# Two transformer-mixer layers on one core: VectorE's exponentials begin during layer 0's feed, and its first phase covers 1024 queries

## The chip, the cores and the metric

One NeuronCore of a Trainium2 chip runs the whole program. The metric is device time in microseconds (us), the median of several runs. The engines are TensorE (PE, with its weight loads PEld), VectorE (DVE), ScalarE (ACT), GpSimd (POOL) and SyncE (SP, which issues most DMAs). Each runs its own list of instructions in order, and waits on semaphores for the others.

## The reference

Two equal layers over x of 2048 tokens by 640, in bf16. Each layer adds attention with 32 heads of width 20 to x, and then a mixer, an MLP that works across tokens.

```python
def _A_ref(x, wqkv, wo):
    qkv = (x @ wqkv).reshape(B, S, 3, H, Dh).transpose(2, 0, 3, 1, 4)
    q, k, v = qkv[0], qkv[1], qkv[2]
    p = softmax(einsum("bhqd,bhkd->bhqk", q, k) * Dh ** -0.5)
    return einsum("bhqk,bhkd->bhqd", p, v).transpose(0, 2, 1, 3).reshape(B, S, D) @ wo

def _B_ref(x, w1, b1, w2, b2):
    u = gelu(einsum("bsd,sf->bdf", layernorm(x), w1) + b1)
    return (einsum("bdf,fs->bds", u, w2) + b2).transpose(0, 2, 1)

for _ in range(2):
    x = x + _A_ref(layernorm(x), A_wqkv, A_wo)
    x = x + _B_ref(layernorm(x), B_w1, B_b1, B_w2, B_b2)
```

The scores are 32 x 2048 x 2048 in each layer, and every one needs an exponential.

## The kernel before

**Units and chunks.** Heads go in 8 groups of 4, queries in 4 blocks of 512, keys in 16 tiles of 128. A unit is one block of queries, one group and one tile of keys; it has four chunks, one a head, of 128 keys by 512 queries. A layer has 4·8·16 = 512 units and so 2048 chunks. (In the last block a chunk is cut into two halves of 256 queries over two key tiles; the count is the same.)

**Two ways to an exponential.** PE writes scores (line 687, function `s_matmul`) into PSUM tiles S of three and of two chunks in turn, and ACT turns a whole tile into P with one instruction (line 757, `emit_exp`). Or PE writes one chunk into the PSUM bank Dt, and DVE makes the exponential with integer arithmetic (`ve_admit`, `ve_enqueue`): line 547 moves the chunk into the tile ew, two chunks make a pair, and a pair goes through a shift (line 645, mostly on POOL), a square (line 577), a product (line 581, tile et) and the last step into Pd (line 600, or line 598 where POOL has prepared its first part in line 628). The value products of P and Pd (line 1310) are summed in the PSUM bank acc.

**The planner.** No order is written by hand. While the kernel is built, a loop in `attention` keeps modelled clocks for PE, DVE and ACT, and a coarser one for POOL (`port`), and appends each instruction to its engine's list when the model says that it fits. Score tiles are issued so that ACT never waits; value products and "fills" (projections, transposes, output projection, mixer) go into the gaps, and where nothing is ready PE multiplies zeros (line 746) to keep its clock. `ve_admit` puts a chunk on DVE if DVE's modelled backlog is under 7 us, at least four units ahead of ACT, with a margin of 3.0 us (`VE_MARGIN`) between the planned result and its use. POOL's part runs beside a DVE instruction chosen as host (`ve_shift`, `ve_base`).

**The feed and the early phase.** Layer 0 begins with `TokenFeed`: x is loaded by tiles of 128 tokens, normalized on DVE, transposed on PE, and projected into K, Q and V for the first four groups. Keys appear one block of 512 tokens after another, so no unit order is fixed yet: `extend` picks units from `early_runs`, the early query blocks times four groups, as far as their keys and queries are there (`reach`). Whenever a run is broken off, the sum in acc is transposed (line 794) and kept in KT's rows of groups that are not used yet, and added later (line 802). Once all the keys of the early runs are there, the order of the remaining units is fixed. `early_qbs = (0,)` makes this phase 64 units long in layer 0, `(0, 1)` 128 units, as in layer 1 (`MixFeed`).

**The end of the feed.** `feed_ended` closes the feed's buffers, opens the next ones (`open_late`, among them the four pools of DVE's exponentials: vew, vet, vey, vep) and calls `after_end`: POOL clears the padded output weights wo_pad (line 1481) and issues two small bias loads (lines 182 and 183), SP loads wo_pad with 32 DMAs (line 200), and the second half of V becomes a fill. `ve_admit` does nothing before, as its first condition asks for `late`, nor while the early phase still lasts (`early[0]`).

In layer 1 the feed is the mixer of layer 0, and a last mixer ends the program.

Of the kernel before, what the change touches and what calls it, by code (L numbers as in the profile page):

```python
# [12 lines left out]
BF16 = mybir.dt.bfloat16  # L13
F32 = mybir.dt.float32
I32 = mybir.dt.int32
I16 = mybir.dt.int16
U16 = mybir.dt.uint16
F16 = mybir.dt.float16
# [44 lines left out]
POOL_HOST = 0.45  # L63
POOL_BASE_HOST = 0.45
VEP_BUFS = 4
VE_ADD = (1.22, 1.03, 0.69)
POOL_DMA = 0.9

# [12 lines left out]
def kernel(  # L81
# [141 lines left out]
    def attention(st, x_in_ap, x_mid, uacc_l, feed, feed_stack):  # L223
# [11 lines left out]
            return pp[f"s{w}"].tile([128, w, 512], F32, name="S")  # L235
        ntmp, ptp = st.ntmp, st.ptp
        p1.enter_context(tc.manual_schedule(engines={nc.vector.engine, nc.scalar.engine, nc.gpsimd.engine}))
        late = {}

        def open_late():  # L240
            def pool(name, bufs):
                late[name] = p1.enter_context(tc.tile_pool(name=f"{name}{layer}", bufs=bufs, reuse_waits="tile"))
            pool("xsp", 3 if x_in_ap.dtype == F32 else 2)
            pool("w1sp", 2)
            pool("ustg", 2)
            pool("atp", NG + 4)
            pool("vew", 3)
            pool("vet", 1)
            pool("vey", 2)
            pool("vep", VEP_BUFS)  # L250
        T2 = ntmp.tile([128, 16, 32], BF16, name="T2")
        nc.gpsimd.memset(T2[:], 0.0)
        h2_tiles, tt_state, attnT_tiles = {}, {}, {}
# [250 lines left out]
        def located(n):  # L504
            return cursor[0] >= NH * (n + 1)

        ve_w, ve_P, ve_ready, ve_users, ve_procs = {}, {}, {}, {}, deque()
        ve_state = dict(unit=-1, pair=0, slot=0)

        def ve_admit(t):  # L510
            now = pem["t"] - WAVE
            if (not late or early[0] or cursor[0] >= NCH or Dbank.free > now + 0.02 or
                    backlog(now) > CFG["VE_BACKLOG"]):
                return
            p, slot = ve_state["pair"], ve_state["slot"]
            if slot == 0:
                if len(ve_procs) > 2:
                    return
                done = backlog(now) + 2 * 1.2 + 4.0 + CFG["VE_MARGIN"]
                n = max(cursor[0] // NH + max(CFG["VE_LEAST"], math.ceil(done / 1.8)), ve_state["unit"] + 1)  # L520
                if n >= NU:
                    n = max(cursor[0] // NH + math.ceil((done - CFG["VE_MARGIN"]) / 1.8), ve_state["unit"] + 1)
                if n >= NU and Dbank not in banks:
                    banks.append(Dbank)
                if n >= NU or not unit_ok(units[n], now - 0.1):
                    return
                ve_state["unit"] = n
            n = ve_state["unit"]
            js = {c[1] for c in tiles[t]}
            free = [j for j in range(NH) if (n, j) not in on_dve]  # L530
            c = (n, next((j for j in free if j not in js), free[0]))
            clash = c[1] in js
            on_dve.add(c)
            loc[c] = (p, slot)
            ve_users.setdefault(p, []).append(c)
            ve_shifted.setdefault(p, [])
            Dt = Dbank.alloc()
            s_matmul(Dt[:, :], *c)
            at = pe_wave("S", cells=0.25) if clash else now
            Dbank.free = 1e9  # L540
            if slot == 0:
                ve_w[p] = late["vew"].tile([128, 2, 512], I32, name="ew")
            w = ve_w[p]

            def first(end):
                Dbank.free = end + DVE_TO_PE
                nc.vector.tensor_scalar(out=w[:, slot, :], in0=Dt[:, :], scalar1=127.0 * FIX,  # L547
                                        scalar2=0.0, op0=ALU.add, op1=ALU.max)

            def firsted(end):  # L550
                pieces.append((p, slot, w, end))
                bases.append((p, slot, w, end))
                if slot == 1:
                    ve_enqueue(p, 2, end + DVE_NEXT)
            submit(Proc(2, [(0.69, first, 0.0)], at + PE_TO_DVE, after=firsted))
            ve_state["slot"] = 1 - slot
            if slot == 1:
                ve_state["pair"] = p + 1

        def ve_enqueue(p, k, ready):  # L560
            w = ve_w.pop(p)
            wh = w[:, 0:k, :].rearrange("p a b -> p (a b)").bitcast(I16).rearrange("p (c two) -> p c two", two=2)
            frac = wh[:, :, 0].bitcast(U16)
            whole = wh[:, :, 1]
            box = {}

            def shifted(end):
                todo = [x for x in range(k) if x not in ve_shifted[p]]
                c0, c1 = 512 * todo[0], 512 * (todo[-1] + 1)
                for x in list(pieces):  # L570
                    if x[0] == p:
                        pieces.remove(x)
                shift(nc.vector, ve_y_of(p)[:, c0:c1], frac[:, c0:c1])

            def squared(end):
                y = ve_y_of(p)[:, 0:512 * k]
                nc.vector.tensor_tensor(out=y, in0=y, in1=y, op=ALU.mult)  # L577

            def mantissa(end):
                box["t"] = late["vet"].tile([128, 1024], I16, name="et")  # L580
                nc.vector.scalar_tensor_tensor(out=box["t"][:, 0:512 * k], in0=ve_y.pop(p)[:, 0:512 * k],  # L581
                                               scalar=MANT_C * MANT_K ** 2, in1=frac, op0=ALU.add, op1=ALU.mult)

            def expo(end):
                Pd = ve_result(p)
                ve_P[p] = Pd
                ve_ready[p] = end + DVE_TO_PE
                ve_procs.popleft()
                for x in [x for x in bases if x[0] == p]:
                    bases.remove(x)  # L590
                based = ve_based.pop(p, [])
                parts = [range(k)] if len(based) in (0, k) else [[x] for x in range(k)]
                for part in parts:
                    lo, hi = 512 * part[0], 512 * (part[-1] + 1)
                    bits = Pd[:, 0:k, :].rearrange("p a b -> p (a b)").bitcast(I16)[:, lo:hi]
                    t = box["t"][:, lo:hi]
                    if part[0] in based:
                        nc.vector.tensor_tensor(out=bits, in0=bits, in1=t, op=ALU.add)  # L598
                    else:
                        nc.vector.scalar_tensor_tensor(out=bits, in0=whole[:, lo:hi], scalar=128.0, in1=t,  # L600
                                                       op0=ALU.mult, op1=ALU.add)
            steps = [(0.15 + 0.27 * (k - len(ve_shifted[p])), shifted, 0.0, True)] if len(ve_shifted[p]) < k else []
            cost = VE_ADD[min(2, len(ve_based.get(p, [])) + 2 - k)]
            steps += [(0.69, squared, 0.0, True), (1.22, mantissa, 0.0, True), (cost, expo, 0.0, True)]
            proc = Proc(4, steps, ready, allow=lambda me: ve_procs[0] is me and
                        (len(me.steps) > 1 or p in ve_results or p - VEP_BUFS not in ve_users))
            proc.pair, proc.ready = p, max([ready] + ve_shifted_at.get(p, []))
            ve_procs.append(proc)
            dvm["procs"].append(proc)
# [2 lines left out]

        def ve_result(p):
            if p not in ve_results:
                ve_results[p] = late["vep"].tile([128, 2, 512], BF16, name="Pd")
            return ve_results[p]

        def ve_base(at):
# [19 lines left out]

        def ve_y_of(p):
            if p not in ve_y:  # L640
                ve_y[p] = late["vey"].tile([128, 1024], F16, name="ey")
            return ve_y[p]

        def shift(engine, out_ap, in_ap):
# [754 lines left out]
        for k_, v_ in dict(dvm=dvm, acm=acm, pem=pem, Proc=Proc, submit=submit, ln_proc=ln_proc, t_fill=t_fill,  # L1399
                           add_fill=add_fill, when=when, v_fill=v_fill, proj_fill=proj_fill, enqueue_qproj=enqueue_qproj,  # L1400
                           kready=kready, vready=vready, base=base, rest=rest, tready=tready, s_start=s_start, KT=KT,
                           Dbank=Dbank, misc=misc, spare=spare, warm_bank=warm_bank, acc_free=acc_free, pe_wave=pe_wave,
                           pump=pump, open_psum=open_psum, tables=[]).items():
            setattr(cx, k_, v_)
        feed.begin(cx)
        feed_ended()
        t = 0
# [44 lines left out]

    class TokenFeed:
        groups = 4
        early_qbs = (0,)
        act_helps = True
        act_free = 0.0
        warm_until = 5.6
# [115 lines left out]
    class MixFeed:  # L1574
        groups = 4
        early_qbs = (0, 1)
        act_helps = True
        act_free = 0.0
        warm_until = 0.0
# [283 lines left out]
```

## Time and profile before

| what | value |
|---|---|
| median of 3 runs | 1757.26 us (1757.2 to 1757.28) |
| the profiled execution | 1757.27 us |
| its span, first to last instruction | 1755.5 us |
| granted clock of TensorE | 1.0 |
| instructions in the span | 43109 |
| layer 0: first exponential on ACT starts, last one ends | 16.05 us, 819.9 us |
| layer 1: first exponential on ACT starts | 856.46 us |
| first exponential step on DVE starts | 109.43 us |

The profile is one execution. "Busy" counts the time in which an engine runs an instruction, waits excluded; a group's line gives the source line, engine, operation, tiles written and read, the count, and after the bars the busy time with the mean of one instruction in ns, and the idle time ahead of them with what ended most of it. In the table of stages each row has the stretch, its length, then busy us and count of instructions for PE, PEld, DVE, ACT and POOL, the granted clock, the share of the DMA engines and GB/s. A row of the order of time has the start, the duration and, in square brackets, the idle time before it.

### The profile page before, as it was taken

The page shows a single profiled execution, that of the slowest core. Times are in us where ns is not written, and L with a number is a line of the kernel's source. Part 1 is how long each engine was busy: PE and PEld are TensorE (multiplying, and loading weights), DVE is VectorE, ACT ScalarE, POOL GpSimd, SP SyncE. Part 2 cuts the span into 40 slices and gives each one's busy share as a digit, 9 for nine tenths or more (in the row PEclk, how much of TensorE's full clock was granted, in tenths as well). Part 3 has the DMA queues.
Part 4 walks back from the last instruction along what each step waited for, and adds up shares of the span by engine and source line. Part 5 has one row for each costly group of instructions (what it writes and reads, how often), then busy time and mean ns, then how long its engine had stood idle before and what let it go on. Part 6 is the DMA issues. An engine that isn't in the chain of part 4 may idle for free.

```text
span 1755.5 us, 43109 instructions
## 1 busy us (share of the span) xinstructions
PE 1670.5 (95%) x17783; PEld 666.8 (38%) x17864; DVE 1521.2 (87%) x2468; ACT 1668.4 (95%) x1502; POOL 577.3 (33%) x921
## 2 busy tenths in 40 slices
PE   8999999999999999999999999999999999999999
PEld 3333233333333344444444433233333333444455
DVE  7479999999999999998543469999999999999973
ACT  8999999999999999999779999999999999999970
POOL 2124442343444343342000023434434442434310
PEclk9999999999999999999999999999999999999999
DMA  4200000000112100133322100001001220101445
GB/s 117 37 4 1 1 1 2 20 28 2 35 53 82 39 25 25 39 86 108 116 78 74 55 21 1 1 2 39 24 1 61 82 72 9 62 2 40 120 124 176
DMA packets 103013, 81.85 MB, mean 47 GB/s; under 512 B 50976, under 2 KB 87456, under 8 KB 102816
## 3 DMA queue, kind: packets, MB, share of 16 engines
q1 hardware_dynamic: 97280, 71.22, 13.7%
q0 software_dynamic: 5536, 7.88, 1.5%
q8 instruction: 139, 2.28, 0.6%
q14 instruction: 58, 0.48, 0.1%
HBM read 55.48 MB, written 23.59 MB: 45 GB/s over the span
## 4 chain that ended last, share of the span: by engine, by line
ACT 50%; PE 24%; issue 21%; DVE 3%; POOL 0%; DMA 0%; another core or an unknown queue 0%; SPq 0%; ACTq 0%; POOLq 0%; DVEq 0%
ACT P L757 50%; PE S L687 7%; PE acc L1310 3%; PE misc L1052 2%; PE ya L1746 2%; PE acc L746 2%; PE misc L1161 1%; PE misc L1101 1%; PE um L1733 1%; PE ya L1755 1%; DVE et L581 1%; DVE ew L547 1%; PE yb L1746 1%; PE misc L1665 0%; PE Dt L1161 0%
## 5 line engine op out<-in xcount | busy, mean ns | idle before, releaser
L757 ACT ACTIVATE P<-S 128x1536 bf16<-128x1536 f32 (+2 forms) x1434 | 1620.8, 1374 | 13.2 <-PE S L687 12.7
L687 PE MATMUL S<-QTq,KT 32*128 32x512 bf16 (+1 forms) x4452 | 577.5, 337 | 65.2 <-ACT P L757 47.1
L645 POOL TENSOR_SCALAR ey<-ew 128x512 f16<-128x512 uint16 x515 | 318.2, 618 | 727.3 <-DVE et L581 323.4
L687 PEld LDWEIGHTS <-KT 32*128 32x128 bf16 x5124 | 233.2, 91 | 524.9 <-issue 497.2
L547 DVE TENSOR_SCALAR ew<-Dt 128x512 int32<-128x512 f32 x516 | 351.5, 681 | 19.8 <-PE Dt L687 13.6
L1310 PE MATMUL acc<-P,Vaug 128*32 128x512 bf16 (+1 forms) x4448 | 363.5, 343 | 0.3 <-DVE Vaug L367 0.3
L746 PE MATMUL acc<-zr,zw 128*32 128x512 bf16 x4232 | 325.5, 382 | 1.2 <-POOL zr L154 1.2
L581 DVE SCALAR_TENSOR_TENSOR et<-ey,ew 128x1024 int16<-128x1024 f16 x258 | 321.4, 1246 | 2.9
L628 POOL TENSOR_SCALAR Pd<-ew 128x512 int16<-128x512 int16 x303 | 186.4, 619 | 142.3 <-DVE et L581 37.4
L687 PE MATMUL Dt<-QTq,KT 32*128 32x512 bf16 (+1 forms) x672 | 198.2, 332 | 0.0
L577 DVE TENSOR_TENSOR ey<-ey 128x1024 f16<-128x1024 f16 x258 | 184.4, 715 | 0.5
L1310 PEld LDWEIGHTS <-Vaug 128*32 128x32 bf16 x5120 | 102.4, 94 | 176.7 <-issue 162.4
L746 PEld LDWEIGHTS <-zw 128*32 128x32 bf16 x4452 | 110.8, 96 | 96.1 <-issue 50.9
L600 DVE SCALAR_TENSOR_TENSOR Pd<-ew,et 128x1024 int16<-128x1024 int16 (+1 forms) x138 | 138.2, 1002 | 0.3
L598 DVE TENSOR_TENSOR Pd<-Pd,et 128x1024 int16<-128x1024 int16 (+1 forms) x183 | 117.1, 640 | 6.3 <-POOL Pd L628 3.8
L887 POOL TENSOR_TENSOR rstd<-veps,mhalf 128x1 f32<-128x1 f32 x60 | 47.6, 793 | 227.0 <-DVE veps L885 197.3
L1310 PE MATMUL acc<-Pd,Vaug 128*32 128x512 bf16 (+1 forms) x672 | 101.3, 334 | 1.2 <-DVE Pd L598 1.2
L1161 PE MATMUL misc<-hh,wq_pad 128*128 128x512 bf16 x273 | 82.4, 383 | 2.6 <-issue 1.7
L1052 PEld LDWEIGHTS <-w1st 128*128 128x128 bf16 x672 | 52.8, 97 | 57.8 <-issue 45.2
L794 DVE STREAM_TRANSPOSE T<-acc 128x512 f32<-128x512 f32 (+1 forms) x81 | 56.4, 696 | 20.3 <-PE acc L1310 19.8
L1101 PE MATMUL misc<-wo_pad,attnT 128*128 128x320 bf16 x384 | 73.0, 302 | 0.5 <-DVE QTq L369 0.3
L1052 PE MATMUL misc<-x1last,w1st 128*128 128x320 bf16 x384 | 72.9, 302 | 0.0
(145 smaller groups left out, 1184.2 us busy)
## 6 DMA issues: line engine op xcount, KB each, us to landing
w2s<-in_B_w_dram SPq DMA_DIRECT2D x16, 768.0 KB
uacc<-ustg POOLq DMA_DIRECT2D x24, 320.0 KB, 2.6
x1in<-xd SPq DMA_DIRECT2D x24, 320.0 KB
w1st<-in_B_w_dram SPq DMA_DIRECT2D x24, 256.0 KB
xd<-x2s SPq DMA_DIRECT2D x16, 320.0 KB
xin<-xd SPq DMA_DIRECT2D x16, 320.0 KB
w1st<-in_B_w_dram SPq DMA_DIRECT2D x24, 192.0 KB
xd<-x1s SPq DMA_DIRECT2D x12, 320.0 KB
```

Source lines behind the costliest of these rows:

```text
L547: nc.vector.tensor_scalar(out=w[:, slot, :], in0=Dt[:, :], scalar1=127.0 * FIX, scalar2=0.0, op0=ALU.add, op1=ALU.max)
L577: nc.vector.tensor_tensor(out=y, in0=y, in1=y, op=ALU.mult)
L581: nc.vector.scalar_tensor_tensor(out=box["t"][:, 0:512 * k], in0=ve_y.pop(p)[:, 0:512 * k], scalar=MANT_C * MANT_K ** 2, in1=frac, op0=ALU ...
L598: nc.vector.tensor_tensor(out=bits, in0=bits, in1=t, op=ALU.add)
L600: nc.vector.scalar_tensor_tensor(out=bits, in0=whole[:, lo:hi], scalar=128.0, in1=t, op0=ALU.mult, op1=ALU.add)
L628: after_vector(nc.gpsimd.tensor_scalar(out=bits, in0=whole, scalar1=128.0, scalar2=0.0, op0=ALU.mult, op1=ALU.add))
L645: return engine.tensor_scalar(out=out_ap, in0=in_ap, scalar1=MANT_K / FIX, scalar2=-MANT_K * MANT_S, op0=ALU.mult, op1=ALU.add)
L687: pe(nc.tensor.matmul(out_ap[:, c0:c0 + w], lhsT=KT[32 * j:32 * j + 32, g, kt * 128:(kt + 1) * 128], rhs=get_QT(st, qb)[32 * j:32 * j + 32 ...
L746: pe(nc.tensor.matmul(bank[32 * j:32 * j + 32, 0:w], lhsT=zw[:], rhs=zr[:, :, 0:64].to_broadcast([128, w // 64, 64]), start=start, stop=st ...
L757: nc.scalar.activation(out=P[:, 0:ncs, :].rearrange("p a b -> p (a b)"), in_=St[:, 0:ncs, :].rearrange("p a b -> p (a b)"), func=ACT.Exp, ...
L1052: pe(nc.tensor.matmul(t[:, 0:w], lhsT=w1_of[(p, ft)][:, sti, :], rhs=rows_in[sti][:, c0:c1], start=(sti == 0), stop=(sti == n_in - 1)))
L1310: pe(nc.tensor.matmul(acc[32 * j:32 * j + 32, a0:a0 + w], lhsT=Vaug[:, (kt * H + hh_) * VW:(kt * H + hh_) * VW + 32], rhs=P[:, slot, c0:c0 ...
```

## The change

Three things in layer 0. The four pools of DVE's exponentials are opened ahead of the feed, at the other end of SBUF (`side="right"`), and `ve_admit` asks for them in place of `late`. While the early phase lasts, DVE may take a unit that is not yet in the list: the new function `far` lets the list be extended up to it, if at least six units more than that (`VE_SPARE`) can be reached. And `early_qbs` of `TokenFeed` becomes `(0, 1)`. For layer 1 the flag `ve_early` is off; its pools are opened where they were, at the other end of SBUF.

```diff
+VE_SPARE = 6
...
-        late = {}
+        late, ve = {}, {}
+
+        def open_ve():
+            for name, bufs in (("vew", 3), ("vet", 1), ("vey", 2), ("vep", VEP_BUFS)):
+                ve[name] = p1.enter_context(tc.tile_pool(name=f"{name}{layer}", bufs=bufs, side="right", reuse_waits="tile"))
...
             pool("atp", NG + 4)
-            pool("vew", 3)
-            pool("vet", 1)
-            pool("vey", 2)
-            pool("vep", VEP_BUFS)
+            if not feed.ve_early:
+                open_ve()
...
+        def far(n, now):
+            if not feed.ve_early:
+                return False
+            now -= 0.1
+            if sum(reach(qg, now) for qg in early_runs) < n + VE_SPARE - len(units):
+                return False
+            while len(units) <= n:
+                if not extend(now):
+                    return False
+            return True
...
-            if (not late or early[0] or cursor[0] >= NCH or Dbank.free > now + 0.02 or
+            if (not ve or over() or Dbank.free > now + 0.02 or
                     backlog(now) > CFG["VE_BACKLOG"]):
                 return
...
+                if early[0] and n >= len(units) and not far(n, now):
+                    return
...
-                if n >= NU and Dbank not in banks:
+                if n >= NU and not early[0] and Dbank not in banks:
                     banks.append(Dbank)
...
+        if feed.ve_early:
+            open_ve()
         feed.begin(cx)
...
     class TokenFeed:
         groups = 4
-        early_qbs = (0,)
+        early_qbs = (0, 1)
+        ve_early = True
...
     class MixFeed:
         groups = 4
         early_qbs = (0, 1)
+        ve_early = False
```

More of the change, by code (lines that the diff above doesn't have):

```diff
@@ L541, in ve_admit @@
             if slot == 0:
-                ve_w[p] = late["vew"].tile([128, 2, 512], I32, name="ew")
+                ve_w[p] = ve["vew"].tile([128, 2, 512], I32, name="ew")
             w = ve_w[p]
@@ L579, in mantissa @@
             def mantissa(end):
-                box["t"] = late["vet"].tile([128, 1024], I16, name="et")
+                box["t"] = ve["vet"].tile([128, 1024], I16, name="et")
                 nc.vector.scalar_tensor_tensor(out=box["t"][:, 0:512 * k], in0=ve_y.pop(p)[:, 0:512 * k],
@@ L614, in ve_result @@
             if p not in ve_results:
-                ve_results[p] = late["vep"].tile([128, 2, 512], BF16, name="Pd")
+                ve_results[p] = ve["vep"].tile([128, 2, 512], BF16, name="Pd")
             return ve_results[p]
@@ L640, in ve_y_of @@
             if p not in ve_y:
-                ve_y[p] = late["vey"].tile([128, 1024], F16, name="ey")
+                ve_y[p] = ve["vey"].tile([128, 1024], F16, name="ey")
             return ve_y[p]
```

## The prediction

> **What bounds the kernel now.** I read the page's engine line first, then the table of stages over layer 0, then ScalarE's exponentials by form and their waits, and last VectorE's and GpSimd's order of time around the end of the feed.
>
> ```profile
> PE 1670.5 (95%) x17783; PEld 666.8 (38%) x17864; DVE 1521.2 (87%) x2468; ACT 1668.4 (95%) x1502; POOL 577.3 (33%) x921
> ```
> ```profile
> 40.00:80.00 40.00, 37.54 (x294) 14.42 (x296) 18.63 (x36) 40.00 (x37) 7.75 (x5) 1.00 0.27 30
> 80.00:120.00 40.00, 37.16 (x316) 13.65 (x321) 23.50 (x41) 40.00 (x36) 5.91 (x10) 1.00 0.07 15
> 120.00:160.00 40.00, 38.36 (x332) 13.96 (x333) 38.91 (x63) 40.00 (x37) 17.44 (x29) 1.00 0.01 1
> ```
> ```profile
> L757 ACT ACTIVATE P<-S 128x1536 bf16<-128x1536 f32 x355 | 565.3, 1592 | 1.7 <-PE S L687 1.5
> L757 ACT ACTIVATE P<-S 128x1024 bf16<-128x1024 f32 x355 | 416.2, 1173 | 0.0
> L757 ACT ACTIVATE P<-S 128x512 bf16<-128x512 f32 x1 | 0.7, 685 | 0.0
> ```
>
> PE and ACT tie at 95%, but PE's share holds zero waves that fill its gaps. The stages decide: in 40 to 120 us ACT (fourth engine figure) is busy in all of it, DVE (third) for 42.1 of 80 us, and from 120 us both are full. The forms are those of 16 to 820 us, layer 0's exponentials: 803.7 us busy for 355·3 + 355·2 + 1 = 1776 chunks of 128x512, that is 0.4525 us a chunk, and idle only 1.7 us, of which 1.5 lie ahead of the first. So ACT is the bound of layer 0 from 16.05 us to its last exponential at 819.9; what shortens the layer is a chunk that ACT need not take. The layer has 2048 chunks; DVE takes the other 272, none before about 109 us.
>
> **The exponentials.** The planner writes every engine's order out when the kernel is built, so the instruction order of the changed kernel gives counts, though no times. In layer 0 ACT has 354 exponentials of three chunks and 353 of two: 1768 chunks, eight fewer, and DVE 280. DVE's first stands after ACT's 37th exponential, where it stood after the 83rd. At the point where ACT has taken 400 chunks (16 + 400·0.4525 = 197 us) DVE has 46 against 34; the remaining layer gives four of these twelve back (234 against 238). That the early phase is larger than that gain suggests: DVE is full from 120 us on anyway, so only the idle of 40 to 120 us can be used, and that once.
>
> ACT's saving: the durations in the rows overlap. A pair takes (803.7 − 0.4)/355 = 2.263 us, the two durations sum to 2.765, so each hides 0.251. Net, three chunks cost 1.341, two 0.922, one 0.434. One, two and one of them go: 1.341 + 2·0.922 + 0.434 = 3.62 us; by proportion 8·0.4525 = 3.62. All of it lies on the path.
>
> **What DVE and POOL take over.** Rows of section 5:
>
> ```profile
> L547 DVE TENSOR_SCALAR ew<-Dt 128x512 int32<-128x512 f32 x516 | 351.5, 681 | 19.8 <-PE Dt L687 13.6
> L581 DVE SCALAR_TENSOR_TENSOR et<-ey,ew 128x1024 int16<-128x1024 f16 x258 | 321.4, 1246 | 2.9
> L577 DVE TENSOR_TENSOR ey<-ey 128x1024 f16<-128x1024 f16 x258 | 184.4, 715 | 0.5
> ```
>
> A pair costs DVE 2·0.681 + 0.715 + 1.246 and about 0.99 for the last step ((138.2 + 117.1)/258, lines 600 and 598): 4.3 us, 2.2 a chunk. Twelve early chunks are 26 us, in 37.9 us of idle; covered. Seven shifts move from POOL to DVE, at most 7·0.68 us, where DVE has slack or the plan counted it; nothing. POOL gains 14 of line 628 at 0.62 us, 8.7 us on an engine a third busy.
>
> **PE, and the larger first phase.** A chunk on DVE costs PE the same score and value products. The partial sums do not grow: transposes of the accumulator 89 → 88, additions 27 → 26; Q projections for the second block of queries only come earlier. In the order, between ACT's 20th and 110th exponentials, 80 zero matmuls are left (116 before), 20 waves of four in some 102 us: PE still has gaps to fill between ACT's tiles, so it keeps up. Three more re-issued score chunks and six more zero waves are fillers; nothing. Layer 1's orders are the same on all engines, so layer 1 and the last mixer cost nothing different; the buffers at the other end of SBUF only move addresses. Behind layer 0's last exponential stand about as many value products as before (24 against 26) and two fewer products of the mixer; ±0.3 us, as the last tile is of three chunks in place of one.
>
> **One thing is moved that the diff does not show.** The feed's end clears wo_pad on POOL and issues two bias loads there. Before, POOL had nothing else:
>
> ```profile
> 41.86 4.36 POOL L1481 MEMSET wo_pad<- 128x5120 bf16 x1
> 46.16 1.24 POOL L182 DMA_DIRECT2D b_t<-in_B_b_dram  x1
> 47.40 1.17 POOL L183 DMA_DIRECT2D b_t<-in_B_b_dram  x1
> 110.21 0.62 POOL L645 TENSOR_SCALAR ey<-ew 128x512 f16<-128x512 uint16 x1 [61.64 <-DVE ew L547]
> ```
>
> In the changed order these 6.77 us stand between a line-645 shift and the same pair's line-628 halves, near ACT's 92nd exponential: 16 + 228·0.4525 = 119 us, so from some 120 to 127. The planner's POOL clock has no term for them. Queued behind are two halves of 0.62, done at 128.2; the DVE addition that reads them stands after the 101st exponential, 16 + 253·0.4525 = 130.5. So the POOL queue is late, but about 2 us before DVE asks; nothing, or up to 6.8 us of DVE without that gap. The 32 wo_pad loads on SP wait for the clearing and move from 46 to some 125 us; behind them on SP are loads for an output projection whose first product starts at 335 us. Nothing.
>
> The second danger is DVE itself, next to a POOL instruction:
>
> ```profile
> 126.39 0.62 POOL L645 TENSOR_SCALAR ey<-ew 128x512 f16<-128x512 uint16 x1 [2.78 <-DVE et L581]
> ```
> ```profile
> 126.55 0.99 DVE L598 TENSOR_TENSOR Pd<-Pd,et 128x1024 int16<-128x1024 int16 x1
> 42.25 0.69 DVE L367 CAST KT<-misc 128x512 bf16<-128x512 f32 x1 [1.03 <-PE misc L1161]
> 44.40 0.49 DVE L367 CAST Vaug<-Dt 128x320 bf16<-128x320 f32 x1 [1.46 <-PE Dt L1185]
> ```
>
> Line 598 in this form takes 0.69 at the median; started inside a POOL instruction with 0.46 us to go it took 0.31 more: it waits for POOL's end, less 0.15. Evacuations from PSUM (0.69 and 0.49, both inside the clearing) do not. In the changed order the clearing meets lines 581, 598 and 600, each with two SBUF inputs. From the row, such an operation would wait up to 4.36 − 0.15 = 4.2 us; from below, nothing, since no row shows a two-input operation beside a clearing. I take nothing and keep both ends. The Trainium skill, "SBUF — State Buffer", section "Who interferes with whom", says that a Vector instruction with two SBUF inputs contends with a GpSimd instruction that reads SBUF, not with one that only writes it; by that rule the cost is nothing, and the sum stays at −3.6 us, where the row's law carried over would give up to +0.6. The wait behind line 645 agrees with its first half (0.31 us); no run here shows the second.
>
> **Sum.** The profiled execution took 1757.27 us (span 1755.5, 1.8 around it), the median 1757.26. 1757.27 − 3.62 = 1753.65; with a tenth for a new small wait, 1753.7.
>
> **Rivals.** (a) The clearing holds DVE. It is one event; everything behind on DVE (two exponential steps, a Q evacuation, a V evacuation, an accumulator's transpose) is up to 4.2 us late. Against the loss stand the planner's 3.0 us of margin (VE_MARGIN) between a planned result and its use: 4.2 − 3.0 = 1.2 us lost with all of it in hand, 4.2 with none: 1754.9 to 1757.9. For it: the row of 0.99. Against it: no two-input operation is seen beside a clearing.
>
> (b) The feed starves ACT: slower. K, Q and V evacuations now queue on DVE behind lines 581 and 600 (1.25 us each), keys come late, and ACT runs out of ready units. Layer 1's feed shows the price, from the waits of ACT over the whole span:
>
> ```profile
> ACT P L757 <- PE S L687: 12.7, 5, 8.3
> ```
>
> One such wait of 8.3 us gives 1753.7 + 8.3 = 1762.0, all of them some 1766. It decides from where the stock of ready units is used up: a unit is four chunks, 1.81 us of ACT, and a DVE unit is only placed ahead with six to spare (VE_SPARE), some 10.9 us. An evacuation would have to be delayed by that much, which speaks against it; layer 0's feed shows no such wait.
>
> (c) Part of the gain is returned in small waits of ACT where one group of heads ends and the next begins, or behind the last tile: 1 to 2.5 us, 1754.7 to 1756.2. For it: DVE has no idle left after 120 us to recover in. Against: over 700 us ACT waits for nothing now.
>
> That the change does not move the work is excluded by the counts.
>
> **How the numbers follow.** Forecast 0.66 (its own range 1753.2 to 1754.2), (a) 0.12, (c) 0.08, (b) 0.11, a better end than 1753.0 in 0.03. The range 1753.0 to 1757.6 leaves out (b), the end of (a) and the better end, under 2 in 10. The bound of 0.2%, about what a measurement of this kernel can tell from no change, is 3.5 us: 1753.75, inside the forecast's own range, a little to its better side. Of 0.66 I count 0.43 below it, and the 0.03: faster 0.46. Same: 0.23 + 0.12 + 0.08 = 0.43. Slower 0.11, all of (b).
>
> **What would show it.** 707 exponentials in layer 0 with ACT idle under 2 us between the first and the last, the last ending near 816.3 us; DVE in 40 to 120 us near 65 of 80 us; line 581 beside the clearing at 1.2 us and not 5. Wrong if ACT waits for PE's S for over 1 us in 40 to 140 us, if a DVE operation near 120 us takes several us, or if layer 1 is not the same length.

## The result and the profile after

The changed kernel takes 1754.11 us (median of 22 runs, 1754.03 to 1755.9), the kernel before in the same sessions 1757.22 us (22 runs, 1757.09 to 1757.93). The ratio is 0.9983, with an interval of 0.9977 to 0.999: 3.11 us or 0.18% faster. That is 0.4 us above the forecast, inside the range, and just on the inner side of the bound of 0.2%. Line numbers from here on are those of the changed kernel, in which the exponential on ACT is line 773 and DVE's steps are lines 563 to 616. The profiled execution took 1754.05 us (span 1752.3).

The engine line of the profile after, and the stages over layer 0 (window, its length, busy time and instructions of PE, PEld, DVE, ACT and POOL, granted clock, then the DMA share and GB/s):

```profile
PE 1677.7 (96%) x17891; PEld 663.4 (38%) x17891; DVE 1534.9 (88%) x2491; ACT 1665.0 (95%) x1498; POOL 592.0 (34%) x936
```
```profile
40.00:80.00 40.00, 38.66 (x312) 13.66 (x312) 26.97 (x49) 39.99 (x37) 8.12 (x12) 1.00 0.03 10
80.00:120.00 40.00, 38.05 (x316) 13.56 (x315) 33.90 (x51) 40.00 (x37) 14.30 (x24) 1.00 0.07 15
120.00:160.00 40.00, 36.97 (x330) 14.28 (x323) 38.30 (x66) 40.00 (x37) 18.93 (x23) 1.00 0.22 22
```

ACT is as full as before, while DVE has gone from 42.1 to 60.9 us of the 80 between 40 and 120 us. From 120 to 160 us it is nearly full in both kernels (38.9 and 38.3 of 40 us). The gain comes from the DVE time used before 120 us, once. ACT's exponentials of layer 0 by form, and the order of time at the end of the layer:

```profile
L773 ACT ACTIVATE P<-S 128x1536 bf16<-128x1536 f32 x354 | 561.3, 1586 | 2.1 <-PE S L703 1.8
L773 ACT ACTIVATE P<-S 128x1024 bf16<-128x1024 f32 x353 | 411.5, 1166 | 0.0
```
```profile
799.36 17.46 ACT L773 ACTIVATE P<-S 128x1536 bf16<-128x1536 f32 x15
853.26 21.84 ACT L773 ACTIVATE P<-S 128x1536 bf16<-128x1536 f32 x19 [0.43 <-PE S L703]
```

There are 354 and 353 exponentials in place of 355, 355 and a single one: 1768 chunks, eight fewer. The last one ends at 799.36 + 17.46 = 816.82 us, where it was 819.9, and layer 1 starts 3.2 us earlier, at 853.26 in place of 856.46.

**Where the 3.1 us come from.** I took the end of each of ACT's instructions from the trace. From one end to the next it is 1.3435 us at the median for a tile of three chunks, 0.9165 for two and 0.491 for one. What a step takes above its median is a small wait. The table gives these sums for all ten kernels (us; "last one ends" is counted with the first exponential's start set to 16.05 us in each, as it lies between 15.93 and 16.14; "seam" is from layer 0's last exponential to the end of layer 1's first, "layer 1" from the end of its first exponential to that of its last).

| kernel | ACT chunks, layer 0 | last one ends | small waits | seam | layer 1 |
|---|---|---|---|---|---|
| before | 1776 | 819.93 | 0.98 | 37.99 | 826.71 |
| after | 1768 | 816.89 | 1.61 | 37.90 | 826.68 |
| e1_one_block | 1774 | 819.52 | 1.49 | 38.70 | 826.70 |
| e2_no_early_start | 1778 | 821.64 | 1.84 | 37.90 | 826.67 |
| e3_clear_reads | 1768 | 822.69 | 7.41 | 37.90 | 826.67 |
| e4_clear_three_times | 1768 | 823.71 | 8.43 | 37.90 | 826.67 |
| e5_one_zero_tile | 1768 | 816.07 | 0.79 | 37.90 | 826.35 |
| e6_before_one_zero_tile | 1776 | 819.87 | 0.92 | 37.98 | 826.35 |
| e7_clear_early | 1768 | 816.91 | 1.63 | 37.90 | 826.70 |
| e8_candidate | 1768 | 816.79 | 1.51 | 38.12 | 826.15 |

After against before: the eight chunks (one tile of three, two of two, one of one) save 1.3435 + 2·0.9165 + 0.491 = 3.67 us; small waits give back 1.61 − 0.98 = 0.63; the seam is 0.09 shorter. The sum is −3.13, against −3.11 measured.

### The profile page after: what moved, and what is told of

It is laid out like the page before. It is cut to its first block, busy times and chain, and to the rows that moved or that the text cites. A ratio compares the mean times of both kernels' runs of the same rounds, so it can differ in the third digit from the quotient of the medians.

```text
span 1752.3 us, 43289 instructions
## 1 busy us (share of the span) xinstructions
PE 1677.7 (96%) x17891; PEld 663.4 (38%) x17891; DVE 1534.9 (88%) x2491; ACT 1665.0 (95%) x1498; POOL 592.0 (34%) x936
## 4 chain that ended last, share of the span: by engine, by line
ACT 50%; PE 25%; issue 22%; DVE 2%; DMA 1%; POOL 0%; SPq 0%; ACTq 0%; DVEq 0%
ACT P L773 50%; PE S L703 7%; PE acc L1326 4%; PE misc L1068 2%; PE ya L1766 2%; PE misc L1177 2%; PE acc L762 2%; PE um L1753 1%; PE Dt L1177 1%; PE ya L1775 1%; PE yb L1766 1%; DMA w2s<-in_B_w_dram 1%; PE misc L1117 0%; PE misc L1685 0%; PE misc L1201 0%
## 5 line engine op out<-in xcount | busy, mean ns | idle before, releaser
L773 ACT ACTIVATE P<-S 128x1536 bf16<-128x1536 f32 (+1 forms) x1430 | 1617.4, 1369 | 13.5 <-PE S L703 13.0
L703 PE MATMUL S<-QTq,KT 32*128 32x512 bf16 (+1 forms) x4449 | 575.6, 337 | 60.9 <-ACT P L773 44.4
L703 PEld LDWEIGHTS <-KT 32*128 32x128 bf16 x5127 | 229.6, 91 | 524.6 <-issue 497.0
L563 DVE TENSOR_SCALAR ew<-Dt 128x512 int32<-128x512 f32 x524 | 357.0, 681 | 22.3 <-PE Dt L703 14.8
L597 DVE SCALAR_TENSOR_TENSOR et<-ey,ew 128x1024 int16<-128x1024 f16 x262 | 325.6, 1243 | 2.8
L644 POOL TENSOR_SCALAR Pd<-ew 128x512 int16<-128x512 int16 x317 | 196.8, 627 | 161.6 <-DVE et L597 42.4
L593 DVE TENSOR_TENSOR ey<-ey 128x1024 f16<-128x1024 f16 x262 | 188.3, 719 | 1.4 <-POOL ey L661 0.3
L616 DVE SCALAR_TENSOR_TENSOR Pd<-ew,et 128x1024 int16<-128x1024 int16 (+1 forms) x134 | 134.6, 1005 | 0.6
L614 DVE TENSOR_TENSOR Pd<-Pd,et 128x1024 int16<-128x1024 int16 (+1 forms) x189 | 121.8, 645 | 5.8 <-POOL Pd L644 3.8
L1177 PE MATMUL misc<-hh,wk_pad 128*128 128x512 bf16 x255 | 74.0, 383 | 0.0
```

The costliest lines, as they stand in the source:

```text
L644: after_vector(nc.gpsimd.tensor_scalar(out=bits, in0=whole, scalar1=128.0, scalar2=0.0, op0=ALU.mult, op1=ALU.add))
L703: pe(nc.tensor.matmul(out_ap[:, c0:c0 + w], lhsT=KT[32 * j:32 * j + 32, g, kt * 128:(kt + 1) * 128], rhs=get_QT(st, qb)[32 * j:32 * j + 32 ...
L773: nc.scalar.activation(out=P[:, 0:ncs, :].rearrange("p a b -> p (a b)"), in_=St[:, 0:ncs, :].rearrange("p a b -> p (a b)"), func=ACT.Exp, ...
L1177: pe(nc.tensor.matmul(t[:, :], lhsT=wpad[:, dt_, g, :], rhs=hT[:, dt_, tb * 512:(tb + 1) * 512], start=(dt_ == 0), stop=(dt_ == NDT - 1)))
```

## Experiments

**The two halves alone.** The change does two things. The first two experiments do one each. In the first, DVE starts early but the first phase covers 512 queries:

```diff
-        early_qbs = (0, 1)
+        early_qbs = (0,)
```

> DVE's early start alone: the early phase stays at 512 queries. Its instruction order has 1774 chunks on ACT in layer 0 (before 1776, changed 1768). Theory (the time follows ACT's chunks in layer 0, 0.46 us each): 1757.2 - 0.9 = 1756.3 us, small waits of ACT 0.3 us either way. Rival (the early start is what pays, the longer phase only shuffles work): most of the 3.1 us, 1754.5 us.

Measured: 1757.68 us, 1.0003 of before (0.9994 to 1.0011). ACT has 1774 chunks, two fewer than before: −0.9 us. It was given back in two places that neither the theory (1756.3) nor the rival (1754.5) had named. One is a wait of 0.97 us at 122.6 us, which the waits of ACT in layer 0 show as one for a P buffer that value products had not yet read:

```profile
ACT P L773 <- PE acc L1326: 0.9, 1, 0.9
```

The other is the seam, 0.7 us longer. Twelve products of the mixer stand behind layer 0's last exponential there, 4 in the kernel before and 2 in the changed one; that these cause it fits, but was not tried alone.

In the second, the phase covers 1024 queries and DVE starts where it used to:

```diff
-        ve_early = True
+        ve_early = False
```

> The phase of 1024 queries alone: DVE's exponentials wait for the feed's end as before. 1778 chunks on ACT in layer 0. Theory (chunks set the time): two chunks more than before, 1757.2 + 0.9 = 1758.1 us. Rival (the longer phase itself saves changes of group and waits): 1755 us or less.

Measured: 1758.83 us, 1.0007 (0.9998 to 1.0016), 1.6 us above before by medians. Two more chunks on ACT are 0.9, small waits are 0.9 more, and the seam is 0.1 shorter. That is slower than the theory by 0.7, and the rival (1755 or less) did not occur. So neither half gains anything alone: DVE's share is 274 and 270 chunks with one of them, 272 with none and 280 with both. The reason is read from the planner: DVE works ahead of ACT and takes only units that are settled well before their turn (VE_SPARE). With 512 queries in the early phase few units are ready, and DVE's first step waits until after ACT's 57th exponential, in place of the 37th. The wider phase supplies the units, the early start uses them.

**The clearing beside DVE: rival (a).** In the changed kernel the clearing of wo_pad and the bias loads run where the working put them, 119.9 to 126.6 us. Here are POOL's order of time and DVE's beside it:

```profile
119.90 4.37 POOL L1500 MEMSET wo_pad<- 128x5120 bf16 x1
124.21 1.24 POOL L183 DMA_DIRECT2D b_t<-in_B_b_dram  x1
125.45 1.17 POOL L184 DMA_DIRECT2D b_t<-in_B_b_dram  x1
126.63 1.22 POOL L644 TENSOR_SCALAR Pd<-ew 128x512 int16<-128x512 int16 x2
```
```profile
119.66 1.26 DVE L597 SCALAR_TENSOR_TENSOR et<-ey,ew 128x1024 int16<-128x1024 f16 x1
120.95 0.43 DVE L614 TENSOR_TENSOR Pd<-Pd,et 128x512 int16<-128x512 int16 x1
121.29 0.68 DVE L616 SCALAR_TENSOR_TENSOR Pd<-ew,et 128x512 int16<-128x512 int16 x1
125.10 0.57 DVE L661 TENSOR_SCALAR ey<-ew 128x512 f16<-128x512 uint16 x1
130.12 0.68 DVE L614 TENSOR_TENSOR Pd<-Pd,et 128x1024 int16<-128x1024 int16 x1
```

Lines 614 and 616 start inside the clearing with two SBUF inputs each and take 0.43 and 0.68 us: no wait. To see whether this is because a memset reads nothing, the next kernel writes the same zeros to the same bytes as a copy from a small tile of zeros:

```diff
-            nc.gpsimd.memset(wo_pad[:], 0.0)
+            nc.gpsimd.tensor_copy(out=wo_pad[:].rearrange("p g (a b) -> p (g a) b", b=32),
+                                  in_=zw[:].unsqueeze(1).to_broadcast([128, NG * D // 32, 32]))
```

> Beside the changed kernel: wo_pad is cleared by a copy from the zero tile zw, so that POOL's instruction reads SBUF, in place of a memset that only writes it. The order is otherwise the same. By the port rule (two SBUF inputs against a reading POOL instruction): one of the DVE operations 581, 598 or 600 near 120 us (597, 614, 616 in the changed kernel's numbering) takes POOL's remaining time less 0.15 us longer, 4 us or more; with the planner's 3.0 us of margin ACT loses about 1.2 us or somewhat more, 1755.3 us, without the margin all of 4.2, 1758.3 us. If reading makes no difference: 1754.1 us and all three DVE operations at their usual 1.2, 0.4 and 0.7 us.

Measured: 1759.29 us, 1.001 (1.0002 to 1.0019), 5.2 us above the changed kernel. POOL and DVE in order of time:

```profile
119.93 5.32 POOL L1500 COPY wo_pad<-zw 128x5120 bf16<-128x5120 bf16 x1
```
```profile
119.68 1.26 DVE L597 SCALAR_TENSOR_TENSOR et<-ey,ew 128x1024 int16<-128x1024 f16 x1
120.97 4.55 DVE L614 TENSOR_TENSOR Pd<-Pd,et 128x512 int16<-128x512 int16 x1
126.05 0.68 DVE L372 TENSOR_SCALAR QTq<-Dt 128x512 bf16<-128x512 f32 x1
```

The same line 614 takes 4.55 us in place of 0.43. The copy had 119.93 + 5.32 − 120.97 = 4.28 us to go, and the operation took 4.12 longer: the law read off one row of before, POOL's rest less 0.15, holds to 0.02. So both halves of what the Trainium skill says in "SBUF — State Buffer", section "Who interferes with whom", are shown here: a Vector instruction with two SBUF inputs waits for a GpSimd instruction that reads SBUF (+4.12 us), and not for one that only writes it (+0).

The 4.1 us of DVE cost more than 4.1 us of ACT: in the profiled execution its last exponential ends 5.8 us later, where rival (a) counted on the planner's margin of 3.0, or on none and 4.2 us. The waits of PE and ACT from 120 to 140 us show why the margin does not help:

```profile
PE Dt L703 <- DVE QTq L372: 2.4, 1, 2.4
ACT P L773 <- PE S L703: 4.3, 2, 2.8
```

The margin stands between a DVE exponential and its use. But DVE also empties the PSUM banks Dt and misc. Here the evacuation of Q from Dt (line 372) came late, PE stood 2.4 us in its order at the next score chunk for that bank, and behind this chunk stood ACT's own score tiles. A bank that DVE empties has no margin.

What goes beyond 4.1 us stands beside a second effect, which nobody had reckoned with: TensorE's granted clock. In the changed kernel it is 1.00 here. In this execution it fell at 125.65 us, while PE stood at Dt, and was 0.50 until 135.89, as this stretch shows (the same columns as in the table of stages):

```profile
125.70:135.80 10.10, 9.02 (x48) 1.88 (x47) 7.79 (x13) 4.94 (x5) 3.82 (x5) 0.50 0.82 69
```

PE was busy in 9.02 of these 10.10 us and the trace has 48 matmuls there, where that of the changed kernel has 95; ACT, busy throughout this stretch in the changed kernel, got 4.94 us of work. Three waits of ACT, 2.87, 1.68 and 0.93 us, end at 128.9, 131.5 and 134.7 us, all in it. The eleven runs go the same way. The two shortest, 1757.90 and 1758.12 us, have a mean clock of 0.999 over the span, and are 3.8 and 4.0 us above the changed kernel, which is about what DVE was late. The five longest, 1759.86 to 1760.50 us, have 0.997. So DVE's delay reaches ACT nearly in full, as in rival (a) without the margin, and the rest goes with the lowered clock. No run held the clock fixed, so the split is read from these runs, not shown by a change.

The next kernel lengthens the clearing without making it read: the memset stands there three times.

```diff
             nc.gpsimd.memset(wo_pad[:], 0.0)
+            nc.gpsimd.memset(wo_pad[:], 0.0)
+            nc.gpsimd.memset(wo_pad[:], 0.0)
```

> Beside the changed kernel: the clearing is written three times, 13.1 us on POOL and with the bias loads 15.5 us, so to some 135.5 us. DVE's addition at 130.1 us waits for POOL halves that end near 136.7 us, so DVE is 6.6 us late there. If the margin of 3.0 us covers a late result: ACT loses 3.6 us, 1757.7 us. If it covers nothing: 1760.7 us. If POOL's queue is of no consequence to the end: 1754.1 us.

Measured: 1761.5 us, 1.0025 (1.0014 to 1.0035), 7.4 us above the changed kernel, more than with no margin at all. DVE's order of time, and two of the waits from 120 to 140 us:

```profile
125.14 3.86 DVE L661 TENSOR_SCALAR ey<-ew 128x512 f16<-128x512 uint16 x1
136.93 0.69 DVE L614 TENSOR_TENSOR Pd<-Pd,et 128x1024 int16<-128x1024 int16 x1 [2.68 <-POOL Pd L644]
```
```profile
PE misc L1201 <- DVE Vaug L370: 4.8, 2, 3.4
DVE Pd L614 <- POOL Pd L644: 2.7, 1, 2.7
```

The mechanism that the expectation named is the second line of the waits: the addition on line 614 waits for POOL's halves, now queued behind 13 us of memset and done at 135.67 + 1.22 = 136.89 us, and starts at 136.93 in place of 130.12. But DVE was late before that, from an operation that I had not suspected. The shift on line 661 has one SBUF input, 16 bits wide, and takes 0.43 us at the median; beside the second memset, which reads nothing, it took 3.86 and ended 0.3 us behind it (124.35 + 4.37 = 128.72; 125.14 + 3.86 = 129.00). The two delays do not add up, as the addition had to wait for POOL until 136.89 in any case; but what stands between them on DVE came late too. An evacuation of V started at 129.71 in place of 126.39, and PE stood 3.4 us at misc; a later one came behind the addition. And here too the granted clock fell while PE stood, at 129.16 us, and was 0.50 until 135.99:

```profile
129.20:135.90 6.70, 5.66 (x29) 1.58 (x29) 4.41 (x7) 3.28 (x3) 6.68 (x4) 0.50 0.24 17
```

ACT's last exponential ends 6.9 us later than in the changed kernel, about the 6.8 us by which the addition was late; how much of it POOL's queue, the shift and the clock each hold was not taken apart. The Trainium skill states in the same section of "SBUF — State Buffer" that a Vector instruction in a two-port mode contends with GpSimd, and sets no condition there that GpSimd reads; the shift's row agrees, if the shift runs in that mode, which the trace does not show. In the changed kernel the clearing ends at 124.27 and this shift starts at 125.10: it misses the clearing by 0.8 us.

Last, the clearing and the bias loads go where POOL has nothing else, behind the feed's last normalization (`after_end` keeps the loads of wo_pad and the rest):

```diff
+                if also is not None:
+                    also()
...
+        def clear(self):
+            nc.gpsimd.memset(wo_pad[:], 0.0)
+            setup_biases()
+
         def after_end(self, cx):
-            nc.gpsimd.memset(wo_pad[:], 0.0)
             setup_wo()
-            setup_biases()
...
-                           allow_apply=lambda: len(out_h) < 4, cheap=0.04)
+                           allow_apply=lambda: len(out_h) < 4, cheap=0.04, also=self.clear if tt == NT - 1 else None)
```

> Beside the changed kernel: wo_pad's clearing and the two bias loads stand on POOL right behind the last normalization's rstd, in POOL's idle stretch from 41.8 to 58.4 us. Forecast (the clearing costs nothing where it is now): 1754.1 us, within 0.2 us. Rival (it costs something unseen near 120 us): lower by what it costs, up to 0.6 us.

Measured: 1754.2 us, 0.9984 (0.9975 to 0.9993). The clearing runs at 41.80 us in POOL's order of time, and the time stays that of the changed kernel:

```profile
41.80 4.36 POOL L1502 MEMSET wo_pad<- 128x5120 bf16 x1
```

So the clearing costs nothing where the changed kernel has it. That is an escape by two accidents of its order, though: a memset does not read, and the shift comes 0.8 us late enough.

**The missing half microsecond.** The 0.63 us more of small waits are none of the named dangers. In the changed kernel the larger ones lie at 52, 55, 195, 229, 675, 697.5 and 725 us, between 0.09 and 0.41 us each, spread over the layer. PE's order of time ahead of the one at 229 us:

```profile
226.77 0.39 PE L703 MATMUL S<-QTq,KT 32*128 32x512 bf16 x2
227.09 1.33 PE L762 MATMUL misc<-zr,zw 128*32 128x512 bf16 x12
228.24 0.40 PE L1326 MATMUL acc<-P,Vaug 128*32 128x512 bf16 x4
228.57 0.39 PE L703 MATMUL S<-QTq,KT 32*128 32x512 bf16 x3
```

The twelve zero matmuls are three waves of fillers. They take 228.24 − 227.09 = 1.15 us to the next value product, where the planner counts 0.2155 a wave, 0.65 us. Each wave takes a new tile of misc, which has one bank, so it waits until the wave before it has completed: 0.47 us from start to start. A filler that takes longer than the gap it fills makes ACT wait. The edit lets consecutive waves write one tile:

```diff
-        misc = Bank(lambda: pp["misc"].tile([128, 512], F32, name="misc"))
+        zero_tile = [None]
+        def new_misc():
+            zero_tile[0] = None
+            return pp["misc"].tile([128, 512], F32, name="misc")
+        misc = Bank(new_misc)
...
-                bank = misc.alloc()
+                zero_tile[0] = bank = zero_tile[0] if zero_tile[0] is not None else misc.alloc()
```

> Beside the changed kernel: zero waves that follow each other in the misc bank write one tile, in place of a new tile each. Instruction order and ACT's 1768 chunks stay. Theory: of the 3.67 us that eight chunks are worth, 0.6 us was lost in small waits of ACT, and a part of them stands where three zero waves into misc follow each other, each waiting 0.47 us for the one before where the planner counts 0.22; then the waits of 0.41 us near 697 us and 0.20 us near 229 us go, and the time falls by 0.5 to 1.2 us over both layers, to 1753.3 us. Rival (the small waits come from DVE's results): 1754.1 us and the same waits.

Measured: 1752.93 us, 0.9976 (0.9967 to 0.9985): 1.18 us below the changed kernel and 4.3 below the one before, the lowest median of all. At the same place in PE's order:

```profile
227.08 0.83 PE L767 MATMUL misc<-zr,zw 128*32 128x512 bf16 x12
227.74 0.39 PE L1331 MATMUL acc<-P,Vaug 128*32 128x512 bf16 x4
```

Three waves take 0.66 us, as planned. The waits at 229, 675, 697.5 and 725 us are gone and layer 0's sum falls from 1.61 to 0.79; layer 1 is 0.33 us shorter. Those two make 1.15 of the 1.18. The same edit on the kernel before the change:

> The same edit on the kernel before, to see the change without this loss. If chunks set the time, the distance to the run on the changed kernel is 3.4 to 3.7 us: some 1756.8 us. If the edit gains as much here as there, the distance stays 3.1 us.

Measured: 1756.77 us, 0.9997 (0.9989 to 1.0006). Layer 0 gains 0.06 there, layer 1 0.36, about as much as in the changed kernel: the order before had hardly any such waits in layer 0, so it is the new order that put long runs of fillers into tight gaps. It is that of the longer phase: without the early start, ACT has waits of the same 0.12, 0.41 and 0.09 us at 680, 703 and 730 us. With the edit on both sides the change is worth 1756.77 − 1752.93 = 3.84 us, without it 3.11.

**A combination.** One zero tile, the early clearing, and less room asked of the fillers:

```diff
-    FILL_ROOM=-0.12,
+    FILL_ROOM=-0.2,
```

> One zero tile and the early clearing together, and fills may start with 0.08 us less room (FILL_ROOM -0.2): ACT has 1768 chunks in layer 0 and 1800 in layer 1 (1804 before), with nine mixer products behind layer 0's last exponential in place of two. Theory: 1753.3 - 4 x 0.46 + 7 x 0.09 = 1752.1 us. Rival (fills that start with less room make ACT wait): 1754 us or more.

Measured: 1753.68 us, 0.9979 (0.997 to 0.9987): a miss, 0.7 us slower than one zero tile alone, between the theory (1752.1) and the rival (1754 or more). ACT got new waits: 0.61 us at 376 us in layer 0, and in layer 1 1.19 us at 1049 and 1.15 us at 1055. The waits of ACT over the whole span put the first two of them down to P buffers that value products had not yet read:

```profile
ACT P L778 <- PE acc L1333: 1.8, 3, 1.1
```

Behind the one at 1049 us PE stood too, 1.36 us, and the granted clock was 0.50 from 1050.92 to 1054.33 us, where it is 1.00 in the changed kernel. The wait of 1.15 us lies at the end of it:

```profile
1051.00:1054.30 3.30, 3.30 (x25) 0.82 (x23) 1.31 (x3) 2.67 (x3) 1.53 (x3) 0.50 0.00 0
```

The 0.7 us go with this lowered clock. Four of the eleven runs have a mean clock of 1.000 and took 1752.74 to 1753.11 us, about as long as one zero tile alone (1752.93); seven have 0.999 and took 1753.53 to 1754.02. So even at the full clock the combination gains next to nothing: the four chunks fewer in layer 1 are 1.8 us, and the new waits and a seam 0.2 us longer take them back. Since the early clearing alone moved nothing, the room of the fillers is the likely cause of the new waits; it was not tried by itself.

## Why the prediction came out as it did

- **The bound and the chunks** were right. ACT sets layer 0, 1768 chunks were left to it, and the layer ends earlier by those eight. The saving was put at 3.62 us and is 3.67: the single last chunk was taken at 0.434 and costs 0.491 from end to end.
- **"A tenth for a new small wait"** is the term that was too small: 0.63 us. This is rival (c) in mechanism (gain returned in small waits), below its price of 1 to 2.5 us, and not at the changes of groups where I looked for it. The step that failed is "six more zero waves are fillers; nothing". I counted PE's gaps in matmuls and not in what a wave takes in this trace, 0.47 us in a row in place of the planned 0.22. Without the waves' chain (e5_one_zero_tile against e6_before_one_zero_tile) the saving is 3.84, close to the 3.62 of the sum and a little above it. The total came within 0.4 us because nothing else that was put at nothing went wrong; for the clearing that was partly luck, as the shift shows.
- **DVE's idle**: 60.9 of 80 us busy against 65 forecast. The cover held. Before 120 us ACT waited only 0.12 and 0.10 us, and it does so without the early start as well (e2_no_early_start, at the same 52 and 55 us), so the lines of 1.25 us beside the feed's evacuations cost nothing that shows, and rival (b) did not occur. In the waits of ACT over the whole span the one long wait is still layer 1's:

```profile
ACT P L773 <- PE S L703: 13.0, 6, 8.3
```

- **POOL's moved work** was right: forecast 120 to 127 us, seen at 119.9 to 126.6, with POOL's halves done at 127.85 and DVE asking at 130.12.
- **Rival (a)** was rightly judged not to occur, and its price was wrong. It took VE_MARGIN as a cushion (1.2 us lost of 4.2). With a reading POOL instruction ACT lost nearly all of DVE's 4.1 us: the margin covers DVE's exponentials and not the banks that DVE empties for PE. The uncushioned end, 1757.9, is what the shortest runs of that kernel took (1757.90 and 1758.12). The others took up to 1760.50, beside a granted clock of 0.50 for 10.2 us in the profiled one; a standing PE that is slower afterwards is a cost that the prediction did not have.
- **The tail and layer 1** were right: the seam moved by 0.09 us within ±0.3, layer 1 by 0.03.
- **The bound of 0.2%** fell between forecast and result: a loss of half a microsecond moved the outcome from faster to same. Nearly even chances for the two were what a forecast 0.05 us from that bound could bear.

## What to carry over

When an engine is full from some point on, extra work for it can only come from its idle time before that point; count that, and look for the second condition (here settled units) without which it stays idle. Fillers are not free: read from the trace what one takes in a row, and let consecutive ones share a target. Before counting on a planner's margin, list every buffer that the late engine frees, since a PSUM bank that it empties holds an in-order PE at once. And before calling the rest of a loss unexplained, read the granted clock of that stretch.

## What the hardware showed that was not expected

- Zero waves that each take a new tile of a one-bank PSUM pool run at 0.47 us a wave; into one tile they run at 0.22.
- A DVE shift with a single 16-bit SBUF input waited for a memset on POOL (3.86 us in place of 0.43), while two-input operations (0.43 and 0.68 us) did not wait for the same kind of memset, and did wait for a copy (4.55).
- After PE had stood for a bank (2.45 and 3.44 us in the two kernels with a changed clearing), TensorE's granted clock was 0.50 for 10.2 and 6.8 us, though its mean over the span is still 0.997 and 0.998. In the combination it was 0.50 for 3.4 us, beside a stop of 1.36. With the clock so lowered, 4.1 us lost on DVE cost ACT 5.8. What decides how long it stays low was not tried.
